# FFT convolution and two expert layers on one core: other slots for the second layer's weights and for the first x operands, and one activation table

## The chip, the cores and the metric

The kernel runs on one core of a Trainium2 chip. The metric is the device time of one execution in microseconds (us), lower is better. The engines of the core are TensorE (PE, with its weight loads as PEld), VectorE (DVE), ScalarE (ACT), GpSimd (POOL) and SyncE (SP, which here issues most DMAs). Each takes its instructions in the order in which they were written for it, and an instruction that waits for a semaphore holds up all that stand behind it on its engine.

## The reference

An FFT convolution over the sequence feeds two dense layers in turn. All is float32.

```python
X = rfft(x, axis=1); Y = X * (filt_r + 1j * filt_i)      # x: 2 x 3008 x 256
x = irfft(Y).reshape(6016, 256)
h = x @ w_in                                             # layer 1: 256 -> 2048
g = where(h >= 1, h, where(h <= -1, 0, (h + 1)**2 / 4))
x = g @ w_out                                            # 2048 -> 256
h = x @ w_in2; g = h * sigmoid(h); out = g @ w_out2      # layer 2, SiLU
```

The weights reach the device as 64-bit words of float64 numbers, two 32-bit halves each, and are turned into float32 on the chip.

## The kernel before, in words

The transform is done as two small DFTs by matmuls (47 by 64 points). Float32 products of the layers are made from two parts of each operand: a high part h, rounded for the fast float32 mode of the PE, and a low part l = v - h; a product is then three matmuls (h·h, h·l, l·h). So every operand, weights as well as activations, must be split: ACT copies the high part, and DVE or POOL subtracts.

The whole program is written out by hand against a clock of slots t. `at(t, fn, ...)` enters a piece of work under a slot, and `due(t)` writes out what is entered there, in the order of entry, behind the matmuls of that slot. NB is the slot at which layer 1 begins, Y = NB + 208 the one at which layer 2 begins. In layer 1 a slot is one `up` (six matmuls of one 128-row block of the hidden layer, for up to 470 tokens), the activation and its split, and one `down` of five slots earlier (six matmuls). The last five `down`s of layer 1 are left over to the first group of layer 2.

Layer 2 takes tokens in six pairs of two halves (502 or 500 columns), p, and for each 8 pairs of hidden blocks, j. One `group(p, j)` makes seven products (a Strassen-like scheme, with names A11, S1, B11, T1, ...) in three PSUM banks b, c and d, and between them calls `between[0]` to `between[3]`: each of these writes one `down2` (six matmuls; in the first group the leftover `down`s, two of them in between[0]) and then `due(Y + 4q + i)`, q being the group's number. So slot Y + 1 is between[1] of group 0, Y + 5 that of group 1, and so on. In a group, bank b is read out by ACT three times (`snap` s1, u2, u4) before the next product may be added to it; DVE then makes the blocks c11, c22, c21 from banks and snaps, ACT applies SiLU. The product A22·T4 is added to bank c, so it waits until DVE has read c for the block c22 (L540).

A weight block f of layer 2 goes through four steps: `fetch_weight` (two DMAs by SP into "raw", three buffers), `read_weight` (ACT, L160 and L161), `form_weight` (DVE, L168 to L170, with a scratch "we", then POOL, L171), and `pair_weight(j)` for the two blocks of a pair: four small DVE operations (L414 to L417) that make sums A21+A22 in place and three more in a scratch "ws", then for a, b and ws each an ACT copy (L422) and a POOL subtraction (L423). The scratches "we" and "ws" have the same tag in the pool, with one buffer (bufs=1): whichever comes next waits until the readers of the other are done. The pair j is used first by group j, so the first four groups need their pairs soonest.

The x operands of pair p = 0 are loaded by `load_pair`, summed on DVE by `sum_x` (L451), and split by `split_x2` (ACT L456, DVE L457). T4 overwrites B21's half.

At the start six matmuls on a zeroed bfloat16 tile "warm" run on the PE before the first transform; `dft_sb` (the transform's matrices and signs) is loaded by a DMA that ACT issues.

Of the kernel before, what the change touches and what calls it, by code (L numbers as in the profile page):

```python
# [15 lines left out]
AF = mybir.ActivationFunctionType  # L16
# [77 lines left out]
def tile_fft_conv_moe_moe(  # L94
# [11 lines left out]
    nc = tc.nc  # L106
# [82 lines left out]
    def clear_pads(tag):  # L189
        zps.clear()  # L190
        for j in range(2):
            z = op.tile([128, DC, 32], F32, tag=f"b{j}", name=f"zp{tag}{j}")
            nc.vector.memset(z, 0.0)
            zps.append(z)

    def load_x(i):
        c, b = items[i]
        if b == 0:

            xt[i] = Z[1][:96, c * TS:(c + 1) * TS]  # L200
        else:
            xt[i] = dp.tile([96, TS], F32, tag="x", name=f"x{i}")
        nc.sync.dma_start(xt[i], x[b, c])
# [365 lines left out]
    def at(t, fn, *args):  # L569
        agenda.setdefault(t, []).append((fn, args))  # L570
# [32 lines left out]
    for i in range(HEAD, n):  # L603
        t = B1 + SP * (i - HEAD) // 10
# [11 lines left out]
    Y = NB + W1S  # L616
# [11 lines left out]
        return [pool.tile([128, 512], F32R, tag=f"w{s}", name=f"w{s}2_{i}") for s in "hl"]  # L628

    for j in range(NP):  # L630
        t = Y - 64 + 13 * j if j < 4 else Y - 8 + 6 * (j - 4)
        for i in range(2):
            f = 2 * j + i
            at(t - 7 + 2 * i, fetch_weight, 1, f)
            at(t - 4 + 2 * i, read_weight, 1, f)
            at(t - 4 + 2 * i, form_weight, 1, f)
        at(t, pair_weight, j, store)

    def make_ring():
# [4 lines left out]
        def extra(i):  # L644
# [7 lines left out]
    X = ((load_pair,), (split_x2, "B11"), (split_x2, "B21"), (sum_x, "T1"), (sum_x, "T2"),  # L652
         (split_x2, "T2"), (sum_x, "T3"), (split_x2, "T3"), (split_x2, "T1"), (split_x2, "B22"),
         (sum_x, "T4"), (split_x2, "T4"))
    for t, x_ in zip((-15, -11, -10, -9, -8, -7, -6, -5, -4, -3, -2, -1), X):
        at(Y + t, x_[0], 0, *x_[1:])
    for p in range(1, len(PAIRS)):
        for t, x_ in zip((0, 14, 16, 17, 18, 20, 22, 24, 28, 29, 26, 30), X):
# [6 lines left out]
    warm = dp.tile([128, 512], BF16, name="warm", bufs=1)  # L665
    nc.vector.memset(warm, 0.0)
    ps = hp.tile([128, TS], F32, tag="h", name="warm_ps")
    for _ in range(WARM):
        nc.tensor.matmul(ps, warm[:, :128], warm, start=True, stop=True)
    clear_pads("a")  # L670
    load_x(0)
    load_x(1)
# [38 lines left out]
    for q in range(len(PAIRS) * NP):  # L711
        p, j = divmod(q, NP)
# [65 lines left out]
```

## Time and profile before

| what | value |
|---|---|
| time, median of 3 runs | 1165.84 us (1165.57 to 1167.01) |
| time of the profiled execution | 1165.26 us |
| its span, first to last instruction | 1163.5 us |
| PE busy in the span | 1128.6 us (97%) |
| DVE, ACT, POOL busy | 721.6, 770.2, 237.5 us |
| granted PE clock, mean | 0.999 of full speed |

The span is the time between the first and the last instruction of the trace; 1.76 us of the execution lie around it. "Busy" is the time in which an engine executes something; a PE that is busy 97% of the span leaves some 35 us in which it waits, and the views by time tell where. A bracket at the end of a row of the timeline is the idle time of that engine ahead of the instruction, and what ended it. In this trace group 0 of layer 2 begins at 649.61 us.

### The profile page before, as it was taken

To read this page: it belongs to the slowest core of one execution; us is meant where nothing else is said; L and a number is where in the kernel's file an instruction comes from. 1 tells how busy PE (TensorE), PEld (TensorE's weight loads), DVE (VectorE), ACT (ScalarE), POOL (GpSimd) and SP (SyncE) were. 2 spreads that over 40 slices of the span, in tenths; PEclk is the share of its full clock that TensorE was granted. 3 is DMA by queue.
4 is the path that set the end of the run, shared out by engine and by line. 5 is a ranking of instruction groups with operands and counts; after the bars stand their busy time and mean duration, and the time that the engine had idled before them with its cause. 6 is when DMAs were issued, how large, how long until landed. Compare 5 with 4: busy or idle time off the path is not lost.

```text
span 1163.5 us, 14351 instructions
## 1 busy us (share of the span) xinstructions
PE 1128.6 (97%) x5155; PEld 945.8 (81%) x5155; DVE 721.6 (62%) x1130; ACT 770.2 (66%) x1447; POOL 237.5 (20%) x204
## 2 busy tenths in 40 slices
PE   9789899999999999999999799999999999999998
PEld 4477788888888999888888678888888888888887
DVE  7999756776754454666657875545555555555443
ACT  3577676777766666767767776666666666666655
POOL 5767534646400000221112330000000000000000
PEclk9999999999999999999999999999999999999999
DMA  9733022222000001022012120010200200100000
GB/s 237 207 93 92 17 81 58 82 61 79 14 18 17 1 18 50 1 73 71 18 50 93 54 89 1 27 45 1 71 1 1 71 1 0 37 1 1 36 1 35
DMA packets 31270, 55.29 MB, mean 48 GB/s; under 512 B 3584, under 2 KB 18400, under 8 KB 31200
## 3 DMA queue, kind: packets, MB, share of 16 engines
q1 hardware_dynamic: 27344, 47.98, 14.1%
q10 hardware_dynamic: 3856, 6.40, 1.5%
q8 instruction: 40, 0.66, 0.2%
q14 instruction: 30, 0.25, 0.1%
HBM read 42.05 MB, written 12.32 MB: 47 GB/s over the span
## 4 chain that ended last, share of the span: by engine, by line
PE 81%; DVE 7%; ACT 5%; DMA 2%; issue 2%; POOL 2%; SPq 0%; ACTq 0%; POOLq 0%; DVEq 0%
PE o L371 13%; PE o L373 13%; PE o L372 13%; PE h L338 6%; PE h L340 6%; PE h L339 6%; PE b L462 4%; PE b L463 4%; PE b L464 4%; DVE g L351 2%; PE xp L319 2%; DVE gl L359 2%; PE c L462 2%; PE c L463 2%; PE c L464 2%
## 5 line engine op out<-in xcount | busy, mean ns | idle before, releaser
L371 PE MATMUL o<-gh,wh 128*128 128x470 f32 (+3 forms) x680 | 260.4, 383 | 0.3 <-ACT ob L379 0.3
L359 DVE TENSOR_TENSOR gl<-g,gh 128x470 fp32r<-128x470 f32 (+1 forms) x192 | 142.6, 743 | 189.6 <-ACT gh L357 188.9
L372 PE MATMUL o<-gl,wh 128*128 128x470 f32 (+3 forms) x680 | 258.4, 380 | 0.0
L373 PE MATMUL o<-gh,wl 128*128 128x470 f32 (+3 forms) x680 | 258.3, 380 | 0.0
L357 ACT ACTIVATE gh<-g 128x470 fp32r<-128x470 f32 (+1 forms) x208 | 122.9, 591 | 134.0 <-PE o L373 96.5
L338 PE MATMUL h<-xh,wh 128*128 128x470 f32 (+1 forms) x416 | 157.0, 377 | 9.9 <-DVE g L351 8.4
L340 PE MATMUL h<-xh,wl 128*128 128x470 f32 (+1 forms) x416 | 155.3, 373 | 1.4 <-POOL wl L183 1.4
L339 PE MATMUL h<-xl,wh 128*128 128x470 f32 (+1 forms) x416 | 155.0, 373 | 0.7 <-DVE xl L328 0.7
L485 DVE TENSOR_TENSOR gl<-c,gh 128x502 fp32r<-128x502 f32 (+1 forms) x192 | 128.4, 689 | 32.4 <-ACT gh L484 32.2
L373 PEld LDWEIGHTS o<-gh,wl 128*128 128x128 f32 x680 | 128.7, 189 | 20.8
L371 PEld LDWEIGHTS o<-gh,wh 128*128 128x128 f32 x680 | 128.3, 189 | 21.3 <-ACT ob L379 0.9
L372 PEld LDWEIGHTS o<-gl,wh 128*128 128x128 f32 x680 | 128.4, 189 | 19.6
L351 DVE SCALAR_TENSOR_TENSOR g<-u,h 128x470 f32<-128x470 f32 (+1 forms) x208 | 130.9, 629 | 11.4 <-ACT u L350 11.4
L344 ACT ACTIVATE u<-h 128x470 f32<-128x470 f32 (+1 forms) x208 | 114.4, 550 | 32.5 <-PE h L340 27.9
L350 ACT ACTIVATE u<-u 128x470 f32<-128x470 f32 (+1 forms) x208 | 119.9, 577 | 0.0
L484 ACT ACTIVATE gh<-c 128x502 fp32r<-128x502 f32 (+1 forms) x192 | 113.6, 618 | 2.3
L171 POOL TENSOR_TENSOR wa<-wa,raw 128x512 int32<-128x512 int32 x32 | 48.6, 1520 | 314.8 <-DVE wa L170 264.9
L471 ACT ACTIVATE u<-b 128x502 f32<-128x502 f32 (+1 forms) x96 | 55.7, 580 | 84.4 <-PE b L464 84.4
L478 ACT ACTIVATE c<-c 128x502 f32<-128x502 f32 (+1 forms) x144 | 88.7, 616 | 27.1 <-DVE c L540 26.9
L338 PEld LDWEIGHTS h<-xh,wh 128*128 128x128 f32 x416 | 78.2, 188 | 25.3 <-DVE g L351 14.5
L540 DVE TENSOR_TENSOR c<-c,u 128x502 f32<-128x502 f32 (+1 forms) x48 | 32.6, 680 | 95.5 <-ACT u L471 95.5
L340 PEld LDWEIGHTS h<-xh,wl 128*128 128x128 f32 x416 | 78.2, 188 | 12.1 <-POOL wl L183 2.6
(133 smaller groups left out, 1832.4 us busy)
## 6 DMA issues: line engine op xcount, KB each, us to landing
f<-in_filt_dram SPq DMA_DIRECT2D x64, 192.0 KB, 4.7
raw<-in_moe_w_in_dram SPq DMA_DIRECT2D x32, 256.0 KB, 3.0
raw<-in_moe_w_out_dram SPq DMA_DIRECT2D x32, 256.0 KB, 3.4
xs<-x2d SPq DMA_DIRECT2D x8, 502.0 KB, 4.7
Z<-in_x_dram SPq DMA_DIRECT2D x16, 192.0 KB, 6.3
x<-in_x_dram SPq DMA_DIRECT2D x16, 192.0 KB, 3.2
x2d<-ob ACTq DMA_DIRECT2D x12, 235.0 KB, 2.0
x2d<-ob SPq DMA_DIRECT2D x12, 235.0 KB, 2.3
```

Of the source, the lines that this page charges most:

```text
L338: nc.tensor.matmul(h, wh[:, s], xh[:, k, :t], start=(k == 0), stop=False)
L339: nc.tensor.matmul(h, wh[:, s], xl[:, k, :t], start=False, stop=False)
L340: nc.tensor.matmul(h, wl[:, s], xh[:, k, :t], start=False, stop=(k == 1))
L344: nc.scalar.activation(u, h, AF.Relu, bias=0.5, scale=0.5)
L350: nc.scalar.activation(u, u, AF.Square)
L351: nc.vector.scalar_tensor_tensor(g, u, 1.0, h, ALU.min, ALU.max)
L357: nc.scalar.activation(gh, g, AF.Copy)
L359: engine.tensor_tensor(gl, g, gh.bitcast(F32), ALU.subtract)
L371: nc.tensor.matmul(o[e], wh[:, s], gh, start=first, stop=False)
L372: nc.tensor.matmul(o[e], wh[:, s], gl, start=False, stop=False)
L373: nc.tensor.matmul(o[e], wl[:, s], gh, start=False, stop=last)
L485: return lambda: nc.vector.tensor_tensor(gl, g, gh.bitcast(F32), ALU.subtract), (gh, gl)
```

## The change

Three edits. The conversion of the second layer's weights gets other slots: the pairs 0 to 3 at Y - 100, - 80, - 60, - 40 in place of Y - 64, - 51, - 38, - 25, and the pairs 4 to 7 at Y + 1, + 5, + 9, + 13 in place of Y - 8, - 2, + 4, + 10; fetches, reads and forms keep their distance to their pair (block i of a pair is fetched at t - 7 + 2i, read and formed at t - 4 + 2i). The x operands of p = 0 are summed and split at other slots, three of the eleven now at Y or behind it. And an activation with the SiLU function on one column of "warm" stands on ACT ahead of the first transform.

```diff
@@ -628,7 +628,7 @@
         return [pool.tile([128, 512], F32R, tag=f"w{s}", name=f"w{s}2_{i}") for s in "hl"]
 
     for j in range(NP):
-        t = Y - 64 + 13 * j if j < 4 else Y - 8 + 6 * (j - 4)
+        t = Y - 100 + 20 * j if j < 4 else Y + 1 + 4 * (j - 4)
         for i in range(2):
             f = 2 * j + i
             at(t - 7 + 2 * i, fetch_weight, 1, f)
@@ -652,7 +652,7 @@
     X = ((load_pair,), (split_x2, "B11"), (split_x2, "B21"), (sum_x, "T1"), (sum_x, "T2"),
          (split_x2, "T2"), (sum_x, "T3"), (split_x2, "T3"), (split_x2, "T1"), (split_x2, "B22"),
          (sum_x, "T4"), (split_x2, "T4"))
-    for t, x_ in zip((-15, -11, -10, -9, -8, -7, -6, -5, -4, -3, -2, -1), X):
+    for t, x_ in zip((-15, -12, -11, -10, -9, -7, -6, -4, -1, 0, 1, 2), X):
         at(Y + t, x_[0], 0, *x_[1:])
     for p in range(1, len(PAIRS)):
         for t, x_ in zip((0, 14, 16, 17, 18, 20, 22, 24, 28, 29, 26, 30), X):
@@ -667,6 +667,8 @@
     ps = hp.tile([128, TS], F32, tag="h", name="warm_ps")
     for _ in range(WARM):
         nc.tensor.matmul(ps, warm[:, :128], warm, start=True, stop=True)
+
+    nc.scalar.activation(warm[:, :1], warm[:, :1], AF.Silu)
     clear_pads("a")
     load_x(0)
     load_x(1)
```

The PE's and POOL's instructions stand in the same order as before. What moves stands on DVE, ACT and SP. First DVE where the layers meet, before: from the last split of layer 1 (gl_15) on. c_0 is a block of group 0, c_1 of group 1, we_12 and we_13 the scratch of blocks 12 and 13 (pair 6).

```order
L359 TENSOR_TENSOR gl_15_6405<-g_15_6384,gh_15_6404 128x470 [waits Activation_49]
L525 TENSOR_TENSOR c_0_6418<-d_0_6414,s_0_6412 128x502 [waits Activation_49]
L168 TENSOR_SCALAR we_12_6436<-raw_12_6332 128x512 [waits DMAHW5_49,DMAHW4_49,Pool_49]
L169 TENSOR_SCALAR wa_12_6433<-wa_12_6433 128x512 [waits Activation_49]
L170 SCALAR_TENSOR_TENSOR wa_12_6433<-wa_12_6433,we_12_6436 128x512 [waits DVE_49]
L485 TENSOR_TENSOR gl_0_0_6449<-c_0_6418,gh_0_0_6448 128x502 [waits Activation_49]
L540 TENSOR_TENSOR c_0_6469<-c_0_6460,u_0_6467 128x502 [waits Activation_49]
L168 TENSOR_SCALAR we_13_6480<-raw_13_6399 128x512 [waits DMAHW7_49,DMAHW6_49,DVE_49]
L169 TENSOR_SCALAR wa_13_6477<-wa_13_6477 128x512 [waits Activation_49]
L170 SCALAR_TENSOR_TENSOR wa_13_6477<-wa_13_6477,we_13_6480 128x512 [waits DVE_49]
```

The pair 5 (ws) was made ahead of these rows, and the pair 6 follows behind them.

The same place on DVE with the change, from group 0's c11 up to the blocks 22 and 21; ws is now that of pair 4, we_10 the scratch of the first block of pair 5.

```order
L485 TENSOR_TENSOR gl_0_0_6383<-c_0_6355,gh_0_0_6382 128x502 [waits Activation_49]
L414 TENSOR_TENSOR ws_6394<-wa_8_6276,wa_9_6331 128x128 [waits Pool_49]
L415 TENSOR_TENSOR wa_9_6331<-wa_9_6331 128x128 [waits DVE_49]
L416 TENSOR_TENSOR ws_6394<-wa_9_6331,wa_8_6276 128x128 [waits DVE_49]
L417 TENSOR_TENSOR ws_6394<-wa_8_6276,ws_6394 128x128 [waits DVE_49]
L168 TENSOR_SCALAR we_10_6414<-raw_10_6306 128x512 [waits DMAHW1_49,DMAHW0_49,Pool_49]
L169 TENSOR_SCALAR wa_10_6411<-wa_10_6411 128x512 [waits Activation_49]
L170 SCALAR_TENSOR_TENSOR wa_10_6411<-wa_10_6411,we_10_6414 128x512 [waits DVE_49]
L451 TENSOR_TENSOR xs_1_5984<-xs_1_5984,t_0_6131 128x502
L540 TENSOR_TENSOR c_0_6429<-c_0_6420,u_0_6427 128x502 [waits Activation_49]
L457 TENSOR_TENSOR xr<-xs_1_5984,xr 128x502 [waits Activation_49]
L548 TENSOR_TENSOR c_0_6451<-c_0_6420,u_0_6386 128x502 [waits PE_49]
```

The pair 4 and the form of block 10 stand in one piece, ahead of the sum and the split of T4 and of the block c22 (L540), and L168 waits for POOL.

ACT at the same place, before: from the last split of layer 1 on; s, u, u are the three snaps of group 0.

```order
L471 ACTIVATE s_0_6412<-b_0_6408 128x502
L478 ACT_TABLE_LOAD
L478 ACTIVATE c_0_6418<-c_0_6418 128x502 [waits DVE_49]
L160 ACTIVATE wa_12_6433<-raw_12_6332 128x512 [waits DMAHW5_49,DMAHW4_49]
L161 ACTIVATE raw_12_6332<-raw_12_6332 128x512
L484 ACTIVATE gh_0_0_6448<-c_0_6418 128x502 [waits PE_49,Activation_49]
L471 ACTIVATE u_0_6452<-b_0_6408 128x502 [waits PE_49]
L471 ACTIVATE u_0_6467<-b_0_6408 128x502 [waits PE_49]
L160 ACTIVATE wa_13_6477<-raw_13_6399 128x512 [waits DMAHW7_49,DMAHW6_49,Pool_49]
L161 ACTIVATE raw_13_6399<-raw_13_6399 128x512
```

There a table load stands ahead of the first SiLU, and nothing between the snaps u2 and u4 (the two L471 that follow each other).

ACT with the change, from the same snap s on.

```order
L471 ACTIVATE s_0_6349<-b_0_6345 128x502
L478 ACTIVATE c_0_6355<-c_0_6355 128x502 [waits DVE_49]
L456 ACTIVATE xr<-xs_1_5984 128x502
L484 ACTIVATE gh_0_0_6382<-c_0_6355 128x502 [waits PE_49,Activation_49]
L471 ACTIVATE u_0_6386<-b_0_6345 128x502 [waits PE_49]
L422 ACTIVATE wh_12_6399<-wa_8_6276 128x512 [waits Pool_49]
L422 ACTIVATE wh_13_6403<-wa_9_6331 128x512 [waits DVE_49,Pool_49]
L422 ACTIVATE wh_14_6407<-ws_6394 128x384 [waits DVE_49]
L160 ACTIVATE wa_10_6411<-raw_10_6306 128x512 [waits DMAHW1_49,DMAHW0_49]
L161 ACTIVATE raw_10_6306<-raw_10_6306 128x512
L471 ACTIVATE u_0_6427<-b_0_6345 128x502 [waits PE_49]
L456 ACTIVATE xr<-xs_1_5984 128x502 [waits DVE_49]
```

The load is gone; three copies of pair 4 and the two reads of block 10 stand between the snaps u2 and u4, and the splits of B22 and T4 in the group as well.

Last, ACT at the very start, before:

```order
L769 UNCONDITIONAL_BRANCH [waits barrier_Pool_Activation_PE_DVE_SP_release]
L130 DMA fwd_80<-in_dft_dram 96x128
L673 DMA dft_sb<-in_dft_dram 128x376
L282 ACT_TABLE_LOAD
L282 ACTIVATE s_142<-v_139 64x384 [waits DVE_49]
```

and with the change:

```order
L771 UNCONDITIONAL_BRANCH [waits barrier_Pool_Activation_PE_DVE_SP_release]
L130 DMA fwd_80<-in_dft_dram 96x128
L671 ACT_TABLE_LOAD [waits DVE_49]
L671 ACTIVATE warm<-warm 128x1 [waits PE_49]
L675 DMA dft_sb<-in_dft_dram 128x376
```

The table load and the one-column SiLU, which waits for the PE, now stand ahead of the DMA that loads dft_sb.

## Rows read from the trace of the kernel before

**Rows 1.** The page's busy times by engine, with share and instructions

```profile
PE 1128.6 (97%) x5155; PEld 945.8 (81%) x5155; DVE 721.6 (62%) x1130; ACT 770.2 (66%) x1447; POOL 237.5 (20%) x204
```

**Rows 2.** Timeline of PE, groups 0 to 2: start, duration, instruction, idle before

```profile
649.61 0.39 PE L462 MATMUL b<-xr,wh 128*128 128x502 f32 x1
...
653.07 0.49 PE L462 MATMUL d<-xr,wh 128*128 128x502 f32 x1 [2.62 <-DVE g L351]
...
661.19 0.50 PE L462 MATMUL b<-xr,wh 128*128 128x502 f32 x1 [4.60 <-ACT s L471]
...
670.11 0.39 PE L462 MATMUL b<-xr,wh 128*128 128x502 f32 x1
...
677.26 0.49 PE L462 MATMUL b<-xr,wz 128*128 128x502 f32 x1 [1.53 <-ACT u L471]
...
682.14 0.39 PE L462 MATMUL b<-xr,wz 128*128 128x502 f32 x1
...
692.34 0.39 PE L462 MATMUL b<-xr,wz 128*128 128x502 f32 x1
```

**Rows 3.** Stretch after the long wait: length, busy by engine, PEclk, DMA, GB/s

```profile
661.20:665.50 4.30, 4.30 (x12) 3.55 (x13) 2.83 (x6) 3.99 (x6) 0.54 (x1) 0.60 0.00 0
```

**Rows 4.** Timeline of ACT, slots Y - 1 to Y + 10

```profile
648.52 0.66 ACT L161 ACTIVATE raw<-raw 128x512 int32<-128x512 uint32 x1
649.08 0.61 ACT L456 ACTIVATE xr<-xs 128x502 fp32r<-128x502 f32 x1
...
654.10 0.61 ACT L422 ACTIVATE wh<-wa 128x512 fp32r<-128x512 f32 x1
...
661.16 1.28 ACT L478 ACT_TABLE_LOAD   x1
662.45 0.62 ACT L478 ACTIVATE c<-c 128x502 f32<-128x502 f32 x1
...
673.48 1.28 ACT L422 ACTIVATE wh<-wa 128x512 fp32r<-128x512 f32 x2
...
686.84 0.57 ACT L471 ACTIVATE u<-b 128x502 f32<-128x502 f32 x1
...
688.95 0.62 ACT L422 ACTIVATE wh<-wa 128x512 fp32r<-128x512 f32 x1
```

**Rows 5.** Timeline of DVE: a split beside POOL, a form and a block

```profile
650.72 1.74 DVE L359 TENSOR_TENSOR gl<-g,gh 128x470 fp32r<-128x470 f32 x1
...
679.47 0.42 DVE L168 TENSOR_SCALAR we<-raw 128x512 int32<-128x512 int32 x1
...
680.97 0.68 DVE L548 TENSOR_TENSOR c<-c,u 128x502 f32<-128x502 f32 x1
```

**Rows 6.** Timeline of POOL: an addition, and the last subtraction of three pairs

```profile
650.43 1.52 POOL L171 TENSOR_TENSOR wa<-wa,raw 128x512 int32<-128x512 int32 x1 [4.62 <-ACT u L344]
...
658.87 1.40 POOL L423 TENSOR_TENSOR wl<-ws,wh 128x384 fp32r<-128x384 f32 x1
...
676.76 0.99 POOL L423 TENSOR_TENSOR wl<-ws,wh 128x384 fp32r<-128x384 f32 x1
...
693.47 1.02 POOL L423 TENSOR_TENSOR wl<-ws,wh 128x384 fp32r<-128x384 f32 x1
```

**Rows 7.** Groups by line and shape: busy, mean ns of one, idle before

```profile
L168 DVE TENSOR_SCALAR we<-raw 128x512 int32<-128x512 int32 x32 | 20.3, 635 | 0.0
```

**Rows 8.** Start: timeline of ACT's queue, PE and PEld

```profile
1.19 2.74 PE L669 MATMUL warm_ps<-warm 128*128 128x512 bf16 x6 [1.19 <-DVE warm L666]
1.19 0.45 ACTq L673 DMA_DIRECT2D dft_sb<-in_dft_dram  x1
...
6.74 0.29 PEld L243 LDWEIGHTS s<-t,dft_sb 128*128 128x128 f32 x1 [0.68 <-DVE t L256]
```

**Rows 9.** DMA issues by line: KB each, median us to landing

```profile
dft_sb<-in_dft_dram ACTq DMA_DIRECT2D x1, 188.0 KB, 3.9
```

**Rows 10.** Stretch of the start, columns as in rows 3

```profile
5.00:10.00 5.00, 5.00 (x8) 2.16 (x7) 2.42 (x4) 0.39 (x1) 1.87 (x2) 1.00 1.04 246
```

## The prediction, made before the changed kernel ran

> **What bounds the kernel now.** I read the page's busy times first: PE is busy 97% of the span, DVE 62%, ACT 66% [rows 1]. So an edit counts only where PE waits, or where it makes PE wait. Then the PE's timeline where the layers meet. The first product of group 0 begins at 649.61 us, that of group 1 at 670.11, of group 2 at 682.14, of group 3 at 692.34 [rows 2]: the groups last 20.50, 12.03 and 10.20 us. Group 2 shows no wait, so 10.20 us for its 45 matmuls (0.227 us each) is the full rate. Group 0 has 21 matmuls of 502 columns and 30 of 470, which at that rate per column are 21 x 0.227 + 30 x 0.212 = 11.13 us. So group 0 loses 9.4 us and group 1 1.8 us, 11.2 together. Group 0's loss is a wait of 2.62 for DVE, one of 4.60 for the snap s1 on ACT [rows 2], and a slow stretch behind it, where the granted clock was 0.60 for 4.30 us [rows 3], which is 4.30 x 0.40 = 1.7 us. This 11.2 us is all that the change can win there; behind group 2 PE runs at its full rate, so every microsecond of difference at the junction should stay in the end time.
>
> **The change part by part.**
>
> *Pairs 0 to 3 earlier.* Same work, inside layer 1, one pair per 20 slots. The trace has all four of these there at no PE wait worth a term; I take 0.
>
> *Before Y.* Pairs 4 and 5 leave the slots ahead of Y, and with them the backlog of ACT and DVE. I take 11.2 us as won back in full, and then price what the first groups of layer 2 cost in the new order.
>
> *A new wait on DVE.* Before, a form (L168) never stood in the same slot as a pair. In the 32 of them DVE was idle 0.0 us ahead of L168 [rows 7]. With the change pair j and the first form of pair j + 1 fall in one slot (Y + 1, Y + 5, Y + 9), so L168 stands right behind L417 and waits for POOL. It has to: "we" and "ws" share one buffer, and ws is read until the last L423. How long that is, the trace has three times, from the first L422 of a pair on ACT to the end of its last L423 on POOL: 673.48 to 677.75, 4.27 us; 688.95 to 694.49, 5.54; 654.10 to 660.27, 6.17 [rows 4, 6]. The shortest is the case in which DVE was through its small sums before POOL came. Here DVE starts them a little behind the first copy, so I take 5.0, with 4.27 and 6.17 as ends. Behind L168 are queued L169, L170 and the block c22 (L540); from L168's start to such a block's end the trace has 679.47 to 681.65, 2.2 us [rows 5]. The PE waits for that block at A22·T4.
>
> *Groups 1 and 2.* In group 2 of before the snap u2, with one read ahead of it as here, begins 686.84 - 682.14 = 4.7 us into the group [rows 2, 4]. ACT starts its next instruction about 0.5 us after one begins (648.52 to 649.08 [rows 4]), so the pair's first copy begins at 5.2. Then 5.0 + 2.15: c22 is done 12.35 us into the group. At full rate A22·T4 would begin nine matmuls before the group's end, at 10.20 - 2.04 = 8.16. So each loses 4.2 us; with the ends of the pair, 3.5 to 5.4. A part of this the PE already waits one product earlier, for u4, which stands on ACT behind three copies and two reads.
>
> *Group 0.* In slot Y - 1 ACT has the two reads of block 9 and T1's copy ahead of the last split and s1, five starts of 0.56 us; s1 comes just in time. DVE's last split of layer 1 then meets POOL's L171 of block 9. That lengthens it as at 650.72, where it took 1.74 us beside an L171 of 1.52 [rows 5, 6]. L171 begins about 3.6 us into the group (the reads, then the three operations of the form) and ends at 5.1, the split 0.5 later, c11 0.65 after that: 6.3. SiLU, B22's copy, the high part and u2 follow on ACT, so u2 ends at 8.4 where S1·T1, behind 12 matmuls of 502 and 18 of 470 columns, could begin at 6.5: 1.8 us lost. The pair begins at 8.35; 5.0 for it, 1.5 for L168 to L170, 0.6 each for T4's sum and c22, and 0.7 to 1.3 for T4's subtraction make 16.75 to 17.35. The PE could have been at the second matmul of A22·T4, which reads the subtraction, at 9.4 (19 and 24 matmuls), so the group loses 7.4 to 8.0 in all; I take 7.5. Ends: 5.7 without the meeting and with 4.27, 8.7 with 6.17.
>
> *Group 3.* Pair 7 at Y + 13 has no form behind it. The three copies stand ahead of u4, as those of pair 6 stood ahead of u2 in group 1 of before, which cost a wait of 1.53 [rows 2]; with the ends 0 and 1.5 I take 0.7.
>
> *The table load.* Before it stood at 661.16 for 1.28 us, the SiLU behind it began 0.01 us after its end [rows 4]; it lies in group 0's 9.4 us and is thus already counted as gone.
>
> *The start.* The one-column SiLU waits for the six warm-up matmuls, which end at 1.19 + 2.74 = 3.93 us, and the DMA of dft_sb is behind it on ACT: issued at about 4.1 instead of 1.19 and landing 3.9 us later [rows 8, 9], at 8.0. The first use on PE was at 6.74 [rows 8]: 1.3 us late. The cover is the DMA: its 16 engines are full there (share 1.04 in 5 to 10 us [rows 10]), the same bytes pass, and later x blocks come earlier by what dft_sb leaves free. I take 0, with 1.3 as the other end if that cover is gone; nothing can be won, as the bytes are the same.
>
> **The sum.** Loss with the change: 7.5 + 4.2 + 4.2 + 0.7 = 16.6 us; before 11.2: 5.4 us more. I add nothing for the clock, since no single wait here is as long as 4.60 us; it may cost up to 1.7 for a stretch like that of rows 3. On the profiled execution's 1165.26 us (span 1163.5 and 1.76 around it) that is 1170.7; the median of the runs shown is 0.6 higher, which gives 1171.2, rounded 1171. Low ends: 5.7 + 3.5 + 3.5 + 0 = 12.7, which is 1.5 more than before, 1167.3. High ends: 8.7 + 5.4 + 5.4 + 1.5 = 21, with 1.3 for the start 11.1 more, 1177.
>
> **The rivals.**
>
> *Faster: the new wait is hidden.* If POOL is through with a pair before DVE asks, or c22 is not what A22·T4 waits for, only ACT's own work counts. Group 1: u2 at 4.7, first copy at 5.2, copies 3 x 0.55, reads 2 x 0.55, u4 0.57 make 8.5, where S4·B22 could begin at 7.48 (twelve matmuls before the end): 1.0 lost. The same in group 2, 0 in group 3, and in group 0 1.8 + 1.3 + 0.3 = 3.4: 5.4 us in all, 5.8 less than before: 1160. For it: L168 never waited so far, and the backlog ahead of Y is truly gone. Against it: in none of the three rows is the pair through in under 4.27 us. It decides from the point where the pair takes about 2.2 us less than I take, 2.8, at which the sums are equal. Chance 0.13.
>
> *About even.* The wait is there, but at the short end everywhere (4.27) and the last split of layer 1 does not meet POOL's addition: 12.7 against 11.2, and one or two short waits ahead of Y are gone. 1165 to 1168. For it: with pair 6 the short case did occur. Chance 0.17.
>
> *Slower still by the clock.* The stretch at 0.60 came behind the wait of 4.60 [rows 2, 3]. If the waits of groups 0 to 2 each bring such a stretch, 3 x 1.7 = 5.1 come on top of the sum: 1176. For it: in group 0 the PE has less than 1 us of work between its two longest waits. Against it: the waits of a group are in two pieces. Chance 0.10. The Trainium skill's page "TensorE: Matmul & The Clock Gate" (section "HAM oscillation — how this bites in real kernels") speaks for this one: waits that recur throttle the array anew each time, between its levels 1.2 and 2.4 GHz. By that rule the time is this rival's, by the rows it is the sum's; the trace agrees with it once, at the 0.60 of rows 3.
>
> *That the change does not do what it says* I hold for no case of its own: the order shows one load in place of two.
>
> **How the numbers follow.** Forecast 0.60 (its own range 1167 to 1177), even 0.17, faster 0.13, slower by the clock 0.10. About 0.2%, 2.3 us, is what a measurement of this kernel tells from no change: below 1163.5 is faster, above 1168.2 slower. Of the forecast nearly all is slower, of the even case nearly all within. Faster 0.13, same 0.18, slower 0.69. The range 1164 to 1176 leaves out the faster case and a little at the top.
>
> **What would show it.** In the profile after: idle time of DVE ahead of L168, ended by POOL L423, three times 2 to 3 us; PE waits at S4·B22 for ACT's snap and at A22·T4 for L540 or L457 in groups 0 to 2; no wait ahead of d in group 0; groups 1 and 2 of about 14.4 us each; one table load, near 1.2 us. I am wrong if groups 1 and 2 last under 12 us, if L168 still waits for nothing, or if the first use of dft_sb on PE comes late and layer 1 begins later by the same 1.3 us.

## The result and the profile after

The changed kernel takes 1176.07 us (median of 4 runs, 1175.51 to 1176.62), the kernel before 1166.40 beside it: ratio 1.0083, 95% interval [1.0066, 1.0101]. It is 9.7 us slower; forecast were 5.4. The profiled execution took 1175.55 us, its span is 1173.8 us against 1163.5. The busy times read as in [rows 1]:

```profile
PE 1131.9 (96%) x5155; PEld 948.1 (81%) x5155; DVE 720.9 (61%) x1130; ACT 770.0 (66%) x1447; POOL 235.4 (20%) x204
```

PE is busy 3.3 us longer with the same 5155 matmuls, and idle for 7 us more. Most of both stands where the layers meet. The timeline of PE after, as [rows 2] (start, duration, instruction, idle before and what ended it):

```profile
650.62 0.39 PE L462 MATMUL b<-xr,wh 128*128 128x502 f32 x1
...
659.11 0.49 PE L462 MATMUL b<-xr,wh 128*128 128x502 f32 x1 [1.65 <-ACT u L471]
...
664.67 0.49 PE L462 MATMUL b<-xr,wh 128*128 128x502 f32 x1 [3.33 <-ACT u L471]
...
666.97 0.76 PE L462 MATMUL c<-xr,wh 128*128 128x502 f32 x1 [1.34 <-ACT xr L456]
667.98 0.79 PE L463 MATMUL c<-xr,wh 128*128 128x502 f32 x1 [0.25 <-DVE xr L457]
...
671.34 0.62 PE L462 MATMUL b<-xr,wh 128*128 128x502 f32 x1
...
681.80 0.49 PE L462 MATMUL b<-xr,wz 128*128 128x502 f32 x1 [2.09 <-ACT u L471]
...
683.41 0.79 PE L462 MATMUL c<-xr,wz 128*128 128x502 f32 x1 [0.66 <-DVE c L540]
...
686.98 0.40 PE L462 MATMUL b<-xr,wz 128*128 128x502 f32 x1
...
696.83 0.79 PE L462 MATMUL b<-xr,wz 128*128 128x502 f32 x1 [2.12 <-ACT u L471]
...
701.40 0.38 PE L462 MATMUL b<-xr,wz 128*128 128x502 f32 x1
...
710.27 0.50 PE L462 MATMUL b<-xr,wz 128*128 128x502 f32 x1 [1.21 <-ACT u L471]
...
713.18 0.38 PE L462 MATMUL b<-xr,wh 128*128 128x502 f32 x1
```

Layer 2 begins at 650.62 (before 649.61), and groups 0 to 3 last 20.72, 15.64, 14.42 and 11.78 us against 20.50, 12.03, 10.20 and 10.57. That is 1.01 + 0.22 + 3.61 + 4.22 + 1.21 = 10.27, the difference of the spans; behind group 3 every group agrees to 0.02. The waits of 2.62 at d and 4.60 at S2·T2 are gone. In their place PE waits in each of groups 0 to 3 for u4, ahead of S4·B22, and in groups 0 and 1 once more ahead of A22·T4. Behind these waits the matmuls of groups 0 to 2 are longer (0.76 and 0.79 us instead of 0.39). The stretches behind them, columns as in [rows 3]:

```profile
666.97:672.60 5.63, 5.38 (x13) 4.09 (x14) 3.84 (x7) 3.73 (x7) 0.41 (x1) 0.50 0.13 46
683.40:687.50 4.10, 4.09 (x12) 3.32 (x13) 2.43 (x5) 3.27 (x6) 0.79 (x1) 0.62 0.51 155
696.80:702.00 5.20, 5.17 (x15) 3.82 (x16) 3.45 (x7) 3.24 (x6) 1.29 (x1) 0.68 0.00 0
```

The granted clock is 0.50, 0.62 and 0.68, between its two levels of 1.2 and 2.4 GHz. Why u4 is late, one sees on the other engines in group 1. ACT, answering to [rows 4]:

```profile
675.66 0.57 ACT L471 ACTIVATE u<-b 128x502 f32<-128x502 f32 x1
676.13 0.62 ACT L422 ACTIVATE wh<-wa 128x512 fp32r<-128x512 f32 x1
677.10 0.63 ACT L422 ACTIVATE wh<-wa 128x512 fp32r<-128x512 f32 x1 [0.34 <-DVE wa L415]
679.64 0.52 ACT L422 ACTIVATE wh<-ws 128x384 fp32r<-128x384 f32 x1 [1.91 <-DVE ws L417]
680.07 0.65 ACT L160 ACTIVATE wa<-raw 128x512 f32<-128x512 f32 x1
680.62 0.65 ACT L161 ACTIVATE raw<-raw 128x512 int32<-128x512 uint32 x1
681.18 0.57 ACT L471 ACTIVATE u<-b 128x502 f32<-128x502 f32 x1
```

DVE and POOL in groups 0 and 1, answering to [rows 5, 6], and the group of L168, answering to [rows 7]:

```profile
659.62 0.29 DVE L415 TENSOR_TENSOR wa<-wa 128x128 f32<-128x128 f32 x1
659.94 1.27 DVE L416 TENSOR_TENSOR ws<-wa,wa 128x128 f32<-128x128 f32 x1
661.25 1.24 DVE L417 TENSOR_TENSOR ws<-wa,ws 128x128 f32<-128x128 f32 x1
...
681.28 0.43 DVE L168 TENSOR_SCALAR we<-raw 128x512 int32<-128x512 int32 x1 [1.67 <-POOL wl L423]
...
682.68 0.67 DVE L540 TENSOR_TENSOR c<-c,u 128x502 f32<-128x502 f32 x1
```

```profile
659.66 2.68 POOL L423 TENSOR_TENSOR wl<-wa,wh 128x512 fp32r<-128x512 f32 x2 [3.86 <-ACT wh L422]
663.12 1.00 POOL L423 TENSOR_TENSOR wl<-ws,wh 128x384 fp32r<-128x384 f32 x1 [0.78 <-ACT wh L422]
...
680.24 1.00 POOL L423 TENSOR_TENSOR wl<-ws,wh 128x384 fp32r<-128x384 f32 x1 [0.79 <-ACT wh L422]
```

```profile
L168 DVE TENSOR_SCALAR we<-raw 128x512 int32<-128x512 int32 x32 | 19.9, 622 | 5.0 <-POOL wl L423 5.0
```

Between u2 and u4 ACT copies for the pair and reads the next weight. Its third copy waits 1.91 us for DVE, whose sums L416 and L417 take 1.27 and 1.24 us beside POOL's subtractions instead of 0.29. DVE then waits 1.67 us for POOL ahead of L168, and c22 (L540) comes behind that: at 682.68 + 0.67 = 683.35, 12.0 us into the group.

The start, answering to [rows 8, 9]:

```profile
1.26 1.28 ACT L671 ACT_TABLE_LOAD   x1 [1.26 <-DVE warm L666]
3.96 0.20 ACT L671 ACTIVATE warm<-warm 128x1 bf16<-128x1 bf16 x1 [1.42 <-PE warm_ps L669]
3.97 0.36 ACTq L675 DMA_DIRECT2D dft_sb<-in_dft_dram  x1
...
10.60 1.56 PE L243 MATMUL s<-t,dft_sb 128*128 128x384 f32 x2 [4.67 <-DMA dft_sb<-in_dft_dram]
```

```profile
dft_sb<-in_dft_dram ACTq DMA_DIRECT2D x1, 188.0 KB, 6.5
```

The transfer is issued 2.8 us later and takes 6.5 us to land instead of 3.9; PE waits 4.67 us for it. The first `up` of layer 1 (L338) begins at 60.41 us, before at 58.80: 1.6 later, of which 1.0 is left where layer 2 begins.

### The profile page after: what moved, and what is told of

It is laid out like the page before. It is cut to its first block, busy times and chain, and to the rows that moved or that the text cites. A ratio compares the mean times of both kernels' runs of the same rounds, so it can differ in the third digit from the quotient of the medians.

```text
span 1173.8 us, 14344 instructions
## 1 busy us (share of the span) xinstructions
PE 1131.9 (96%) x5155; PEld 948.1 (81%) x5155; DVE 720.9 (61%) x1130; ACT 770.0 (66%) x1447; POOL 235.4 (20%) x204
## 4 chain that ended last, share of the span: by engine, by line
PE 80%; DVE 5%; ACT 5%; issue 3%; POOL 2%; POOLq 0%; ACTq 0%
PE o L371 13%; PE o L373 13%; PE o L372 13%; PE h L338 6%; PE h L340 6%; PE h L339 6%; PE b L462 4%; PE b L463 3%; PE b L464 3%; PE xp L319 2%; PE c L462 2%; PE c L464 2%; PE c L463 2%; DVE g L351 1%; ACT u L350 1%
## 5 line engine op out<-in xcount | busy, mean ns | idle before, releaser
L359 DVE TENSOR_TENSOR gl<-g,gh 128x470 fp32r<-128x470 f32 (+1 forms) x192 | 139.4, 726 | 194.6 <-ACT gh L357 194.6
L338 PE MATMUL h<-xh,wh 128*128 128x470 f32 (+1 forms) x416 | 156.8, 377 | 9.5 <-DVE g L351 8.0
L471 ACT ACTIVATE u<-b 128x502 f32<-128x502 f32 (+1 forms) x96 | 55.7, 580 | 80.2 <-PE b L464 80.2
L338 PEld LDWEIGHTS h<-xh,wh 128*128 128x128 f32 x416 | 78.2, 188 | 24.1 <-DVE g L351 13.3
L540 DVE TENSOR_TENSOR c<-c,u 128x502 f32<-128x502 f32 (+1 forms) x48 | 32.6, 680 | 91.8 <-ACT u L471 91.8
```

Of the source, the lines that this page charges most:

```text
L338: nc.tensor.matmul(h, wh[:, s], xh[:, k, :t], start=(k == 0), stop=False)
L359: engine.tensor_tensor(gl, g, gh.bitcast(F32), ALU.subtract)
```

## The experiments

Theory: the pairs between u2 and u4 hold ACT, DVE and POOL for 5 us each, PE waits for u4 and c22, and the clock falls behind those waits. Rivals: the start, the new wait of L168, the x slots. Times are medians; g0 to g3 are the groups' lengths in the profiled execution.

**The start and the table load.** The changed kernel with the transfer ahead of the SiLU:

```diff
-    nc.scalar.activation(warm[:, :1], warm[:, :1], AF.Silu)
     ...
     nc.scalar.dma_start(dft_sb, dft[:, 128:])
+    nc.scalar.activation(warm[:, :1], warm[:, :1], AF.Silu)
```

> The changed kernel with one line moved: ACT issues the DMA of dft_sb ahead of the one-column SiLU instead of behind it. Theory (the start is a term of its own): PE's wait of 4.67 us for dft_sb goes, layer 1 begins about 1.6 us earlier, and the whole is 1.6 us shorter, about 1174.5. Rival (what is late at the start is made up later, because DVE bounds the stretch up to 140 us): the wait goes and the time stays at 1176.

1176.02 us, 0.05 less. The wait for dft_sb is gone, layer 2 begins at 649.99, but g2 lasted 15.93, 1.5 longer than in the changed kernel with the same order there. The reverse: the kernel before with the SiLU ahead of the transfer.

> The kernel before with the one-column SiLU alone, issued ahead of the transform table's transfer as the change has it. Theory: the transfer starts 2.8 us later, lands 6.5 instead of 3.9 us after its issue, TensorE waits 4.7 us for it, layer 1 begins 1 to 1.6 us later, and the time is 1167.4 to 1168.0 instead of 1166.4. Rival: the start isn't on the path that sets the end (moving the transfer back in the changed kernel gave 0.05 us), and the time is 1166.4 within 0.5.

1167.50 us (10 runs), ratio 1.0010 [1.0000, 1.0019]: about 1 us, at the edge of what can be told. And the kernel before with the SiLU behind the transfer, so that only the table load moves:

> The kernel before with one line added: the one-column SiLU behind the DMA of dft_sb, so that a single table load stands at the start and none where the layers meet; slots as before. Theory (the load of 1.28 us lay beside PE work): under 0.4 us, 1166.2. Rival (it was on the path of group 0): 1.3 us shorter, 1165.1.

1166.29 us, ratio 1.0001 [0.9992, 1.0010]: the load wasn't on the path. The start is worth 0 to 2 us, likeliest 1. It also scatters: the first `up` of layer 1 began between 58.80 and 61.41 us in the eight profiled executions of kernels with the SiLU behind the transfer, so 1 us in one trace proves nothing.

**The wait of L168.** The changed kernel with a buffer of its own for ws:

```diff
-        s = rawp.tile([128, 384], F32, tag="we", name=f"ws{j}", bufs=1)
+        s = rawp.tile([128, 384], F32, tag="ws", name=f"ws{j}", bufs=1)
```

> The changed kernel with a buffer of its own for ws, so that a form no longer waits for the POOL subtractions of the pair ahead of it. Theory (the shared scratch is on the path): idle time of DVE ahead of L168 falls from 1.67 us to 0 in groups 0 to 2, A22.T4 no longer waits for c22; groups 1 and 2 are 0.9 us shorter each, group 0 about 1.8 us, together 3.6: about 1172.5. The waits at S4.B22 for u4 stay at about 2 us, since they come from ACT's copies and reads. Rival (those copies and reads, with the clock behind them, are all of the loss): under 0.5 us, 1176.

1174.78 us, 1.3 less, where the theory had 3.6. DVE is idle 0.0 us ahead of L168; the waits for u4 stay at 3.33, 2.04 and 2.17. So 5.0 us of idle DVE were worth 1.3 at most (of it 0.4 is an earlier beginning of layer 2 in the profiled execution): ACT's copies hold u4 nearly as late as L168 holds c22.

**The clock.** The changed kernel with 8 matmuls that compute nothing used ahead of S4·B22 in groups 0 to 2:

```diff
+        for _ in range(8 if p == 0 and j < 3 else 0):
+            nc.tensor.matmul(d, up_weight(j, "A11")[0], xop[p, "B11"][0], start=True, ...)
         prod(b, p, j, "S4", "B22", False)
```

> The changed kernel with eight idle matmuls of 502 columns on PE (into bank d, which is read out by then, so that nothing of the output changes) ahead of S4.B22 in each of groups 0 to 2: 1.8 us at full clock, where PE waits 2.1 to 3.3 us in the changed kernel. Theory (the low granted clock behind the waits is a cost of its own, 1.5 to 2.5 us per group): the clock stays near 1.00 behind the filled waits, groups 1 and 2 are about 1.5 us shorter each, group 0 up to 2: about 1171.5. Rival (the waits set the pace and the slow stretches lie in time that PE would wait anyway): no change or up to 1 us longer, 1176 to 1177.

1175.08 us, 1.0 less, with layer 2 beginning 0.95 us later in the profiled execution. Its groups 0 to 2:

```profile
651.57:671.89 20.32, 15.55 (x60) 11.81 (x59) 15.05 (x23) 12.31 (x23) 6.94 (x6) 0.92 0.32 103
671.89:686.29 14.40, 12.59 (x54) 9.84 (x53) 10.81 (x18) 9.95 (x20) 6.25 (x5) 1.00 0.35 109
686.29:700.21 13.92, 12.59 (x54) 9.83 (x53) 11.00 (x18) 9.86 (x19) 6.28 (x5) 1.00 0.34 110
```

In groups 1 and 2 the clock is 1.00 throughout, and they are 1.24 and 0.50 us shorter. That is the clock's price between these two executions; it isn't the same in all. In the run with the transfer first, whose order in these groups is that of the changed kernel, group 2 lasted 15.93 at a mean clock of 0.83, 2.0 more than here. Group 0 kept its slow stretch, behind waits of 1.52 and 1.35 us.

These three versions differ from the changed kernel by 0.05 to 1.3 us. Against the kernel before, each measured beside it, their ratios are 1.0079, 1.0075 and 1.0077, all within the interval of the changed one (1.0083 [1.0066, 1.0101]): that none of the three takes back more than a small part of the 9.7 us is shown, what each is worth exactly isn't.

**Which edit.** The changed kernel with the old weight slots, and with the old x slots:

> The changed kernel with the weights converted at the slots of before: only the slots of the x operands and the one-column SiLU differ from the kernel before. Theory: the new weight slots cost it all but the start; then groups 1 to 3 last 12.0, 10.2 and 10.6 us as before, group 0 about 20.5, and the time is before plus 1.0 us of the late start: 1167.4. Rival: the later x splits cost by themselves (T1's, B22's and T4's splits now stand inside the first group): group 0 is 2 to 4 us longer than 20.5 and the time 1169 to 1171.

> The changed kernel with the x operands of the first token pair split at the slots of before: the weights' slots and the one-column SiLU alone differ from the kernel before. With the kernel before, the changed one and the one with the old weight slots (group 0 20.5, 20.7 and 23.5 us, group 1 12.0, 15.6 and 14.4) it fills a table of two by two. Theory: the pairs at one in every layer-2 group cost about 4 us each in groups 1 and 2 whatever the x slots; groups 1, 2, 3 last 15 to 16, 14 to 14.5 and 11.5 to 12, group 0 18 to 20 (no x copies behind the pair, so no wait for them ahead of A22·T4), and the time is 1174 to 1175. Rival: the x slots are the cost, since the old weight slots left 1174.0: then group 0 falls to 14 or less, and the time to 1169 or less.

```
weight slots  x slots   g0     g1     g2     g3     time
old           old       20.50  12.03  10.20  10.57  1166.4
old           new       23.54  14.37  10.30  10.51  1173.99
new           old       19.81  14.90  13.69  11.85  1173.96
new           new       20.72  15.64  14.42  11.78  1176.07
```

Either edit alone costs 7.6 us (the start's share included), both together 9.7: they don't add. The theory of the first run falls, and its rival is right on group 0, though its time was too low: with pairs 4 and 5 still ahead of Y the late x splits cost 3.0 us there, where PE waits 3.72 for s1 and twice, 0.34 and 0.60, for T4's split, and 2.3 in group 1, where the mean clock is 0.88. Of the 8.6 us that separate this profiled execution from that of the kernel before, 3.2 stand ahead of group 0 and 2.2 of them already ahead of layer 1, so part of its 7.6 is the start's, scatter included. The theory of the second run holds within 0.3 us: at the old x slots the new weight slots cost groups 1 to 3 nearly what they cost in the changed kernel.

**Where the pair stands in the group.** The changed kernel with the pairs one gap later, behind u4 (and T4's sum and split one gap earlier):

```diff
-        t = Y - 100 + 20 * j if j < 4 else Y + 1 + 4 * (j - 4)
+        t = Y - 100 + 20 * j if j < 4 else Y + 2 + 4 * (j - 4)
...
-    for t, x_ in zip((-15, -12, -11, -10, -9, -7, -6, -4, -1, 0, 1, 2), X):
+    for t, x_ in zip((-15, -12, -11, -10, -9, -7, -6, -4, -1, 0, 0, 1), X):
```

> The changed kernel with each late pair issued one gap later, behind u4 and the c22 sum instead of ahead of S1·T1 (and T4's sum and split one gap earlier, so that they are not behind the pair). Theory: the change costs its time because u4 stands on ScalarE behind the pair's copies. Then the waits at S4·B22 (3.33, 2.09 and 2.12 us in groups 0 to 2 of the changed kernel) are gone, and with them the slow clock behind them: groups 1 and 2 fall from 15.64 and 14.42 to 11 to 12 us, the sum of groups 0 to 3 from 62.6 to 53 to 55, the time from 1176.1 to 1167 to 1169. Rival: the pair needs its 5 us of ScalarE and VectorE in every group wherever it stands; now the SiLU of c22 and c12 and the c21 sum are behind it, the banks come free late, the next group's first products wait instead, and the time stays over 1173.

1173.20 us; 13.50, 15.39, 16.10, 13.10. Group 0 gains 7.2 us, groups 2 and 3 lose, and the wait is now for s1 of the next group:

```profile
669.47 0.79 PE L462 MATMUL b<-xr,wz 128*128 128x502 f32 x1 [2.35 <-ACT s L471]
```

The rival named that and was right; the time is at its edge. With the own buffer and the early transfer as well:

> As the one before, and also the sum tile ws in a buffer of its own (so that VectorE's next weight read doesn't wait for GpSimd's last read of it) and the transfer of the transform's table issued ahead of the one-column SiLU. Theory: the three costs add up, so 7 to 9 us of the pair's place, 1.3 us of the buffer (as measured alone) and 0.6 us of the start come off 1176.1: 1165 to 1167, even with the kernel before. Rival: with the pair behind u4 VectorE isn't ahead of anything that TensorE waits for, so the buffer is worth nothing, and the time is that of the kernel with the moved pair less 0.6.

1168.90 us; 13.49, 14.65, 15.33, 12.21. That is 4.3 us under the version before it, though the two edits alone had given 1.3 and 0.05; the rival falls, and the theory's range is missed by 1.9. The two profiled executions differ by 4.0: 1.5 us of it is the later beginning of layer 2 in the other one (650.75 against 649.21), the rest stands in groups 1 to 3.

**How far apart.** The changed kernel with the late pairs six gaps apart:

```diff
-        t = ... Y + 1 + 4 * (j - 4)
+        t = ... Y + 1 + 6 * (j - 4)
```

> The changed kernel with only the spacing of the late pairs different: every sixth gap from the second of group 0 instead of every fourth, so that the fourth stands in group 4. Theory: density of the pairs is the cost; group 0 stays at 20 to 21 (its pair still stands ahead of u4), group 1 falls from 15.6 to 11 to 12, group 2 from 14.4 to 11 to 12, groups 3 and 4 near 11; the time falls from 1176 to 1168 to 1170. Rival: place, not density; a pair that stands in the gap ahead of u4 costs its 4 us each time, and moved to another gap it costs what that gap's copy waits for; time over 1173.

1167.09 us, ratio 1.0003 [0.9992, 1.0014]: this one number takes back 9 us, the whole change. Its groups 0 to 3, with the first pair in the same place as in the changed kernel:

```profile
650.11:667.24 17.13, 13.25 (x52) 10.46 (x51) 12.82 (x20) 11.16 (x21) 5.29 (x5) 0.90 0.24 88
667.24:677.53 10.29, 10.29 (x47) 8.50 (x46) 8.20 (x16) 8.82 (x17) 2.62 (x2) 1.00 0.53 168
677.53:689.23 11.70, 10.57 (x47) 8.32 (x45) 8.11 (x15) 8.68 (x17) 5.04 (x4) 1.00 0.13 38
689.23:701.07 11.84, 10.54 (x47) 8.34 (x45) 10.18 (x16) 9.18 (x18) 4.98 (x4) 1.00 0.36 122
```

Group 0 is 3.6 us shorter than in the changed kernel, with the same pair in the same gap but no weight read beside it. The pairs behind it cost 1.5 to 1.9 us each and no clock (11.70, 11.84 and, in group 5, 12.07 against 10.20); in groups 1 and 2 of the changed kernel they cost 5.4 and 4.2. Is it that pair and read share a gap, or that there is one pair in every group? The changed kernel with the reads one gap earlier:

```diff
+            k = j > 4
-            at(t - 7 + 2 * i, fetch_weight, 1, f)
+            at(t - 7 - k + 2 * i, fetch_weight, 1, f)
...
```

> The changed kernel with the fetch, the read and the forming of the weights of the late pairs 5 to 7 issued one gap earlier each; the pairs stay where the change put them, one in every group. Theory: the cost of groups 1 and 2 is not the pair alone but the next weight's read in the same gap, whose two ScalarE copies (0.65 + 0.65 us) stand ahead of u4 and whose three VectorE steps wait 1.67 us for GpSimd ahead of the c22 sum. Without it groups 0, 1 and 2 last 17 to 18, 11.5 to 12.5 and 11.5 to 12.5 (group 3, which has a pair and no read, lasts 11.78), in place of 20.7, 15.6 and 14.4, and the time falls from 1176 to 1167 to 1169. Rival (density: one pair in every group is too much for ScalarE and VectorE): what leaves one gap comes back in the next, groups 1 and 2 stay over 13.5, and the time is over 1172.

1174.49 us; 21.46, 14.67, 14.29, 11.61. My theory fell, and the rival's numbers came. With the reads ahead, POOL's addition for them runs beside the first of DVE's sums of the pair, and the pair's own first subtraction beside the second; the copy on ACT waits 2.43 us for these:

```profile
677.00 1.54 POOL L171 TENSOR_TENSOR wa<-wa,raw 128x512 int32<-128x512 int32 x1 [7.77 <-ACT gh L484]
```

```profile
677.30 1.40 DVE L414 TENSOR_TENSOR ws<-wa,wa 128x128 f32<-128x128 f32 x1
678.73 1.26 DVE L415 TENSOR_TENSOR wa<-wa 128x128 f32<-128x128 f32 x1
```

At one pair and two reads in four gaps every pair has a read within one gap, so at this spacing no run can tell the shared gap from the density in groups 1 and 2; which of them it is stays open there. Two versions with all three edits and wider spacing, six gaps and eight:

> The kernel with all three edits (pairs behind u4, own buffer for ws, table's transfer first), with the four late pairs at every sixth gap from the third of group 0, instead of every fourth. Theory: a group has room beside its own work for about two thirds of a pair; at one pair in every group ScalarE, VectorE and GpSimd are late for TensorE in each, at one in one and a half groups they catch up between. Groups 0 to 4 then last 13.5, 10.5 to 11, 11 to 12, 11 to 12 and 10.5 in place of 13.5, 14.65, 15.33, 12.21 and 11.38; 1168.9 falls by 7 to 11 us to 1158 to 1162, below the kernel before. Rival: each pair costs its 3 to 4 us wherever it stands, since what it delays is s1 or u2 of the next product; then the time is within 2 us of 1168.9.

1169.42 us; 13.51, 12.80, 12.94, 10.30, then 12.49 and 15.03. The theory fell; the rival's number is right, though not its reason, since group 3 has nothing to pay and group 5 pays 4.7. The gap within the group counts beside the spacing: two of the four pairs, at gaps 8 and 20, stand in between[0] of groups 2 and 5, ahead of u2, and there S1·T1 waits:

```profile
684.04 0.49 PE L462 MATMUL b<-xr,wz 128*128 128x502 f32 x1 [2.44 <-ACT u L471]
...
720.33 0.79 PE L462 MATMUL b<-xr,wh 128*128 128x502 f32 x1 [2.99 <-ACT u L471]
```

The pairs at gaps 7, 13 and 19 of the run with six gaps alone stood in between[1] or between[3].

> As the kernel with the three edits and every sixth gap, but at the gaps 2, 10, 18 and 24 after the junction, so at most one pair in two groups. Theory (room in a group): groups 1 and 3 without a pair at 10.3, groups 2 and 4 near 11 to 12, as good as every sixth or up to 2 us better: 1157 to 1161. Rival: the second token pair's x operands are split in the gaps 14 to 30, and the pairs at 18 and 24 now meet them; then groups 4 to 7 grow by 1 to 3 us each, and it is 2 to 4 us slower than every sixth gap.

1169.18 us; 13.49, 11.80, 10.29, 10.50, 10.70, then 16.12 and 14.94. Its first four groups are the best so far, but with the pairs at gaps 18 and 24, among the second token pair's splits, groups 5 and 6 lose what was won, 5.8 and 4.6 us, more than the rival gave them; the theory's time was missed by 8, and the rival's, 2 to 4 above six gaps, did not come either. So all three edits, with gaps picked one by one: 2, 7, 13, 19; 2, 10, 13, 19; and 2, 10, 15, 21.

> The kernel with all three edits, the late pairs at gaps 2, 7, 13 and 19 after the junction: the first where group 0 lasted 13.5 us, the others where the kernel with every sixth gap from the second had them (its groups 1 to 5: 10.29, 11.70, 11.84, 10.36, 12.07 us). No pair shares its gap with the read of the next weight. Theory (coincidence with the next read, and groups that don't touch one another): groups 0 to 5 last 13.5, 10.3 to 11.5, 11.0 to 11.7, 11.8, 10.4 and 12.1, in sum 69 to 71 against 73.9 of the kernel before, and the time is 1161 to 1164, below the kernel before. Rival (every pair costs its 3 to 4 us wherever it stands): sum 75 or more, time 1168 or more.

1165.27 us, ratio 0.9986 [0.9977, 0.9995], 1.3 above the theory's range: g1 was 14.47 where I added up 10.3 to 11.5. The reads for the pair at gap 7 (gaps 3 and 5) stand right behind the pair at gap 2.

> As the kernel with the late pairs at gaps 2, 7, 13 and 19, but the second at gap 10 (where groups 1 and 2 lasted 11.80 and 10.29 us in the kernel at gaps 2, 10, 18 and 24). Theory: 13.5, 11.8, 10.3, 11.8 to 12.5, 10.4 and 12.1 in groups 0 to 5, a time within 1 us of the version at gap 7, so that the gap of one pair matters less than what shares it. Rival: with the pairs at 10 and 13 only three gaps apart group 3 grows to 14 or more and the time is 2 to 4 us above the version at gap 7.

1165.32 us, ratio 0.9992 [0.9983, 1.0000], the theory's time; but g3 15.53, as the rival said, while g1 and g2, without those reads, gained 3.5 on the version before it. In that group PE waits 2.15 us for s1 and 2.10 for u4, and the clock stays at 1.00:

```profile
685.67:701.20 15.53, 11.11 (x47) 8.19 (x46) 12.30 (x20) 12.46 (x24) 7.24 (x7) 1.00 0.30 99
```

> As the two kernels with all three edits and chosen gaps, with the late pairs at gaps 2, 10, 15 and 21: the first two where they cost least so far (groups 0 to 2 13.5, 11.8 and 10.3 us), the third five gaps after the second instead of three, so that neither its reads (gaps 11 and 13) nor it stand beside another pair. Theory (a pair that has no read or pair within a gap of it ahead of a copy that TensorE waits for costs at most 1.5 us): groups 0 to 6 in sum 13.5, 11.8, 10.3, 10.5 to 11, 11 to 12, 11 to 12.5 and 10.3, 78.4 to 81.2 against 84.2 of the kernel before, time 1162 to 1164.5. Rival: the second token pair's x splits (gaps 14 to 30) take the room, as at gaps 18 and 24, where groups 5 and 6 lasted 16.1 and 14.9; then group 4 or 5 is over 14 and the time 1166 or more.

1163.10 us (8 runs), ratio 0.9973 [0.9962, 0.9983]: 2.6 us below the kernel before and 13 below the changed one. Groups 0 to 6 last 13.50, 11.79, 10.29, 11.90, 12.35, 11.56 and 10.36, in sum 81.75 against 84.2, a little over the theory's 81.2, with the time in its range. (The profiled execution is the slowest of the eight, 1165.08: its layer 2 begins 2.2 us later than in the profile of before.) Groups 1 to 4:

```profile
665.33:677.12 11.79, 10.53 (x46) 8.32 (x45) 7.62 (x14) 10.03 (x20) 3.31 (x3) 1.00 0.54 174
677.12:687.41 10.29, 10.29 (x47) 8.46 (x45) 8.08 (x14) 6.60 (x13) 3.33 (x4) 1.00 0.33 102
687.41:699.31 11.90, 10.73 (x46) 8.32 (x45) 10.31 (x16) 11.28 (x22) 4.71 (x4) 1.00 0.36 111
699.31:711.66 12.35, 10.99 (x46) 8.24 (x45) 10.34 (x18) 8.86 (x18) 5.36 (x4) 1.00 0.05 20
```

None of these loses more than 2.2 us against a full one, and the clock is 1.00 in all of them. This version was picked after others, and which of its three edits it needs wasn't tried one by one.

## Why the prediction was wrong in size

Right were the direction and the place. L168 waited three times, 1.67 us each (forecast 2 to 3); a pair took 676.13 to 681.24, 5.1 us (5.0); the wait at S1·T1 of group 0 was 1.65 (1.8); the second matmul of A22·T4 in group 0 began 17.36 us into it (16.75 to 17.35); c22 of group 1 was done at 12.0 (12.35); one table load of 1.28 us was left.

The step that failed is "I add nothing for the clock, since no single wait here is as long as 4.60 us". The term taken as 0 came out as follows. In group 0 the rest of the group from that second matmul on, 2 matmuls of 502 and 6 of 470 columns, should last 1.73 us and lasted 671.34 - 667.98 = 3.36: 1.6 more. In group 1 the run with idle matmuls gives 1.24: with the clock at 1.00 the group lasted 14.40, the forecast value. In group 2 it gives 0.50; there the forecast was too long by as much. The rival "slower still by the clock" named the mechanism and 1176; I gave it 0.10 because "the waits of a group are in two pieces". That its time came out to 0.1 us is partly luck: it added 5.1 us for the clock, the three figures above make 3.3, and the start and group 3 fill the gap. The Trainium skill's page "TensorE: Matmul & The Clock Gate" (section "HAM oscillation — how this bites in real kernels"), cited there for that rival, tells of a PE that is throttled anew at each recurring wait, in a kernel with longer waits, for DMAs. The three stretches at 0.50 to 0.68 agree with it; group 3 of the changed kernel and the group at 1.00 with waits of 2.15 and 2.10 us don't.

The rest of the miss is the start, taken as 0 and 1.0 in the trace (0 to 2 by the runs), and group 3, 0.7 forecast and 1.6 measured. For the start the prediction had named a sign of being wrong, a late first use of dft_sb and a later layer 1, and it showed: the first use came at 10.60 us and layer 1's first `up` 1.6 us later, so the cover "the same bytes pass" held only in part. The groups and the start lose 10.3 us in the profiled executions, forecast were 5.4; the difference is start 1.0, group 0 2.1 (1.6 of it the clock), group 1 1.2, group 2 0, group 3 0.9, less 0.4 that group 3 of before already lost and I had not counted: 4.8 of 4.9 us.

The measured 1176.07 lies just above the range of 1164 to 1176 and inside the 1167 to 1177 that the forecast's own ends add up to, but not by the terms of its high end, which were a pair of 6.17 us in each group; a pair took 5.1. The turning point of the "faster" rival was worked out wrongly: by its own terms the two sums of groups 1 and 2 meet at a pair of 1.8 us (5.2 + 1.8 + 2.15 - 8.16 = 1.0), not 2.8; nothing hung on it.

One reason was right only in part. I let c22, behind the waiting L168, set groups 1 and 2. With that wait gone the time fell by 1.3 us, not by the 3.6 that I then expected: u4 is about as late by itself, behind ACT's third copy. In my "faster" rival I had put that copy at 0.55 us; its wait of 1.91 for DVE's sums beside POOL was missing, though [rows 5, 6] show what POOL does to DVE.

What stays open: whether the shared gap or the density makes a pair dear in groups 1 and 2; why the same waits lower the clock in one run's group and not in another's (group 1 at 0.89 or 1.00 with waits of 2.35 + 0.75 and 2.37 + 1.53), and how much of the start's 1 us is the change's.

## What to carry to other kernels

Work that is moved out of a tight place needs room, not only another place: look at how much of it falls into each repeat of the loop that takes it, and spread it wider than the loop's own period; then try the place within the period too, since at six gaps the version with two pairs in between[0] took 1169.42 us and the one without 1167.09. Price a copy on one engine with the waits of its inputs, not by its duration. Where an order leaves recurring waits of some 2 us on TensorE, read the granted clock behind them and add it to the sum.

## What the runs showed of the hardware

- In the changed kernel the clock fell to 0.50 to 0.68 behind waits of 2.09 to 3.33 us; with 8 idle matmuls in the wait it stayed at 1.00 in two groups of three, and behind a wait of 1.21 (group 3) it did too. In another version a group with waits of 2.15 and 2.10 us kept 1.00, so the length of the waits alone doesn't tell.
- A 128x128 sum on DVE took 0.29 us without POOL at work (three in a row from 656.25 to 657.20 in the kernel before) and 1.24 to 1.40 beside it.
- The same 188 KB transfer took 3.9 us to land when issued at 1.19 us and 6.5 when issued at 3.97, into full DMA engines (share 1.03 in the stretch from 5 to 10 us, against 0.79 from 1.2 to 5.1 us, where the first one ran).
- Moving one table load of 1.28 us from the junction to the start changed the time by nothing that can be told (ratio 1.0001 [0.9992, 1.0010]).
